# Odd rows' way back split by frequencies modulo 4, with six rows unfolded on GpSimd, and later transfers put behind the first unit's keys

## The chip, the cores and the metric

One core of a Trainium2 chip runs the whole program. The metric is the device time of one execution in microseconds (us). An execution of the kernel before takes about 453 us, so half a per cent is 2.3 us.

## The reference

The input x is 2048 x 640. Two branches work on it, and a gate per row mixes them:

```python
g = sigmoid((x * gate_w).sum(-1))
a = attention(x @ wqkv) @ wo       # 32 heads of 20; query s sees keys s, s-2, ..., s-14
b = irfft2(rfft2(x) * (w_r + 1j * w_i))
return g * a + (1 - g) * b
```

The second branch is a product in the frequency domain: 2048 points along the rows, 640 along the columns. The change touches its last step, the way back along the 640 columns, and the order of transfers ahead of the attention.

## The kernel before

**Tiles.** Row s of x lies on partition p = s // 16 with index j = s % 16, so a "row j" below is a set of 128 rows. Even and odd j have separate queries and keys, since the attention's step is 2.

**Stages.** (1) `qkv`: x times wqkv in eight units u (four column groups hg for even j, four for odd j), in fp32r with three terms each. Each pair of j goes through an `ev` tile to a buffer `qkvd` in DRAM. (2) `attend(par, h)`: 16 attention units in the order of UNITS; each loads its keys `kt`, queries `q` and values `vt` from `qkvd`. The first is kt0a/q0a/vt0a, the second kt0b (both from u = 0), the third kt4a (u = 4). VectorE multiplies and reduces (`pr`, `L`, `o`), GpSimd does softmax pieces and `pv`. Results `o` go to the DRAM buffers `od`. (3) `fold`, `cols`, `freq`: x is folded by symmetry on VectorE (`fx`; two of the folded tiles wait in DRAM as `fd`), transformed along the rows (`z`), along the columns with the table `bt` (matmuls `u`, `v`), multiplied with the weights (`X`, `P`, `s`), and brought back (`g`). (4) `project_even`: attention output of even j (load `ot`, transposes `oTp`, matmuls `woa`, `wob`), to DRAM as `ad`. (5) `spatial(j)`: the way back along the columns with the table `gt` (matmuls `oa`, `ob`, evictions `os` on ScalarE), then the last half transform (`ha`, `hb`). For even j VectorE unfolds it at once into `y`, which is added to `yi` (from `ad`) and written. For odd j ScalarE only stores the halves `ho`. (6) `project_odd(j)`: unfolds `ho` into `ye` and `y`, projects attention, adds the two and writes `out`.

**Tables and symmetry.** PERM orders the 321 column frequencies: even ones first, odd ones after. With cosine and sine parts apart, the even and the odd frequencies of a row give two halves of 161 numbers, and sums and differences of these make 321 and then 640 outputs. In `spatial` a chunk of 128 frequencies that has both kinds takes a matmul of 322 columns, one that has a single kind one of 161.

**What sets the order.** Nothing is issued as it is written. A class `Plan` records every operation, gives each a cost, and searches an order per engine by list scheduling with random trials; operations are then issued engine by engine in that order (all at one line, L655 in the profile). So each engine works through a fixed row of instructions and waits where an operand is missing. SP, ACT and POOL issue DMAs in the same rows as their other work. A change of costs or dependencies redraws the whole order. Buffers are rings of named places: `yr` holds four `y` tiles, `yer` one `ye` tile, banks 0 to 4 of PSUM hold `woa`/`wob` of odd rows.

The lines that the change turns on:

```python
ODD_POOL = tuple(range(1, 16, 2))            # odd rows that GpSimd unfolds
YI_DMA = tuple(range(0, 10, 2))              # even rows added by an accumulating DMA of GpSimd
...
op.busy = max(4 * n / 2400 + 0.006, 0.182)   # the plan's cost of an f32 matmul
...
U.tensor_add(ye[:, :, 0:161], h[:, 0], h[:, 1])
U.tensor_sub(ye[:, 0, 320:160:-1], h[:, 0, 0, 0:160], h[:, 1, 0, 0:160])
U.tensor_sub(ye[:, 1, 320:160:-1], h[:, 1, 1, 0:160], h[:, 0, 1, 0:160])
```

Of the kernel before, what the change touches and what calls it, by code (L numbers as in the profile page):

```python
# [16 lines left out]
S, D = 2048, 640  # L17
# [7 lines left out]
PERM = np.array([0, 320] + list(range(2, 320, 2)) + list(range(1, 320, 2)))  # L25
# [7 lines left out]
def dft_tables():  # L33
# [7 lines left out]
    ke, ko = PERM[:161], PERM[161:]  # L41
    kb = PERM[2:161]
# [9 lines left out]
    def half(n, *ends):  # L52
# [3 lines left out]

    bt = np.zeros((640, 642))
    bt[0:161, 0:161] = np.cos(tau * np.outer(np.arange(161), ke) / D) * half(161, 0, 160)
    bt[161:321, 161:321] = np.cos(tau * np.outer(np.arange(160), ko) / D) * half(160, 0)
    bt[321:480, 323:482] = -np.sin(tau * np.outer(np.arange(1, 160), kb) / D)  # L60
    bt[480:640, 482:642] = -np.sin(tau * np.outer(np.arange(1, 161), ko) / D) * half(160, 159)
    bt = np.concatenate(
        [bt[0:128, 0:161], bt[128:256, 0:321], bt[256:384, 161:482], bt[384:512, 321:642], bt[512:640, 482:642]], 1
    )

    j, k2 = np.arange(16), np.arange(16)
    md = np.zeros((16, 16, 2, 4, 2, 16, 4))
    mf = np.zeros((16, 2, 16, 4, 16, 2, 4))
    for g in range(16):
        for a in range(4):  # L70
            th = tau * np.outer(j, 4 * g + a + 128 * k2) / 2048
# [48 lines left out]
    d = np.arange(161)  # L120
# [5 lines left out]
    gt[0:161, 0:161] = np.cos(tau * np.outer(ke, d) / D) * ck(ke)  # L126
    gt[161:321, 161:322] = np.cos(tau * np.outer(ko, d) / D) * ck(ko) * (d < 160)
    gt[321:480, 322:483] = -np.sin(tau * np.outer(kb, d) / D) * ck(kb) * ((d > 0) & (d < 160))
    gt[480:640, 483:644] = -np.sin(tau * np.outer(ko, d) / D) * ck(ko) * (d > 0)
    gt = np.concatenate(  # L130
        [gt[0:128, 0:161], gt[128:256, 0:322], gt[256:384, 161:483], gt[384:512, 322:644], gt[512:640, 483:644]], 1
    )
    f = np.float32
    return {
        "t_fc": np.concatenate([fc, back[0].T, back[1].T], 1).astype(f),
# [7 lines left out]
class Op:  # L143
    __slots__ = ("i", "eng", "name", "call", "busy", "lat", "size", "preds", "succs", "chain", "tail", "start", "end", "early", "group", "of", "two", "rank")
# [12 lines left out]
class Plan:  # L157
# [5 lines left out]
    def __init__(self, nc):  # L163
        self.ops, self.places, self.past = [], {}, set()
        self.chain = self.group = ""
        self.rank = 0.0
# [57 lines left out]
    def record(self, eng, name, fn, a, k):  # L224
        op = Op()
        op.i, op.eng, op.name, op.chain, op.group = len(self.ops), eng, name, self.chain, self.group
        op.preds, op.succs, op.size, op.early, op.two, op.rank = set(), [], 0, False, False, 0.0
        line = sys._getframe(2).f_lineno
# [14 lines left out]
    def cost(self, op, out, ins, k):  # L243
        n = max(int(np.prod(v.shape[1:])) for v in [out] + ins[:1])
        if op.name == "dma_start":
            op.busy, op.lat = {"SP": 0.45, "ACT": 0.45, "POOL": 1.0}[op.eng], LAND
            op.size = int(np.prod(out.shape)) * 4
            op.early = not hasattr(ins[0].tensor, "tag")
            if self.rank:
                op.rank, self.rank = self.rank, self.rank - 1e3  # L250
        elif op.eng == "PE":
# [5 lines left out]
            else:  # L257
                op.busy = max(4 * n / 2400 + 0.006, 0.182)
# [23 lines left out]
    def order(self):  # L282
# [7 lines left out]
        for op in reversed(ops):  # L290
# [7 lines left out]
            last[key] = op  # L298
        span = max(op.tail for op in ops)
# [213 lines left out]
class Mixer:  # L513
# [17 lines left out]
    def places(self, pp, dr, sb):  # L531
# [35 lines left out]
        self.yr, self.yir = ring("raw3", "raw4", "e0", "ya"), n("f", 2)  # L567
# [10 lines left out]
    def work(self):  # L578
# [45 lines left out]
        self.bt, self.gt = self.one("bt", 1288, tag="e0"), self.one("gt", 1288, tag="e1")  # L624
        S.dma_start(self.bt[:, 0:1284], ins["t_bt"])
# [16 lines left out]
        p.chain = ""  # L642
        staged([self.spatial(j) for j in range(1, NJ, 2)], 2)
# [29 lines left out]
    def load_w(self, st, hg):  # L673
# [4 lines left out]
        for t in range(5):  # L678
# [80 lines left out]
    def attend(self, par, h, step=4):  # L759
# [80 lines left out]
    def fold(self, q):  # L840
# [24 lines left out]
        V.tensor_sub(o[:, :, 0:161], o[:, :, 0:161], bl)  # L865
        V.tensor_sub(f[:, :, 321:480], o[:, :, 1:160], oh[:, :, 159:0:-1])
        V.tensor_add(f[:, :, 480:640], o[:, :, 1:161], oh[:, :, 159::-1])
        V.tensor_add(f[:, :, 0:161], e, eh[:, :, 160::-1])
        V.tensor_sub(f[:, :, 161:321], e[:, :, 0:160], eh[:, :, 160:0:-1])
        self.folded[q] = f  # L870
        if q in STORED:
            p.act.dma_start(self.f_d[:, q], f)

# [26 lines left out]
    def freq(self, g):  # L900
# [25 lines left out]
        row(v[:, 0:161], 3, bt[:, 642:803], False, False)  # L926
        row(v[:, 161:321], 5, bt[:, 1124:1284], False, True)
# [3 lines left out]
        row(u, 1, bt[:, 161:482], True, False)  # L931
        row(u[:, 0:161], 0, bt[:, 0:161], False, False)
        row(u[:, 161:321], 2, bt[:, 482:642], False, True)
# [50 lines left out]
        V.tensor_sub(s[:, d0 : d0 + 319], P[:, 0, 2:], sz[:, 2:])  # L984
# [40 lines left out]
    def spatial(self, j):  # L1025
# [8 lines left out]
        mm(o1[:, 0:322], 1, gt[:, 161:483], True, False)  # L1034
        mm(o1[:, 0:161], 0, gt[:, 0:161], False, False)
        mm(o1[:, 161:322], 2, gt[:, 483:644], False, True)
        mm(o2[:, 0:322], 3, gt[:, 805:1127], True, False)
        mm(o2[:, 0:161], 2, gt[:, 644:805], False, False)
        mm(o2[:, 161:322], 4, gt[:, 1127:1288], False, True)
        os = self.osr.next(f"os{j}", 644)  # L1040
        oq = os.rearrange("p (b a d) -> p a b d", b=2, a=2)
        A.copy(oq[:, 0], o1[:, 0:322].rearrange("p (b d) -> p b d", b=2))
        A.copy(oq[:, 1], o2[:, 0:322].rearrange("p (b d) -> p b d", b=2))
        yield
        h1, h2 = self.ps((3, 4), f"ha{j}"), self.ps((5,), f"hb{j}")
        for i, h in enumerate((h1, h2)):
            for a in range(2):
                T.matmul(
                    h[:, 161 * a : 161 * a + 161],
                    self.fct[:, a],  # L1050
                    os[:, 322 * i + 161 * a : 322 * i + 161 * a + 161],
# [5 lines left out]
        if j % 2:  # L1057
            if j % 4 == 1:
                self.hpair = self.hor.next(f"ho{j}", 2, 2, 2, 161)
            h = self.hpair[:, j % 4 // 2]  # L1060
            A.mul(h[:, 0].rearrange("p b d -> p (b d)"), h1[:, 0:322], ng)
            A.mul(h[:, 1].rearrange("p b d -> p (b d)"), h2[:, 0:322], ng)
# [63 lines left out]
    def project_odd(self, j):  # L1126
# [41 lines left out]
ODD_POOL = tuple(range(1, 16, 2))  # L1168
# [68 lines left out]
```

## Time and profile before

| | |
|---|---|
| median of three runs | 453.15 us (453.03, 453.15, 455.2) |
| the profiled execution | 452.6 us, of which the span is 450.8 us |
| TensorE (PE) busy | 443.1 us |
| VectorE (DVE) busy | 393.0 us |
| GpSimd (POOL) busy | 339.3 us |
| ScalarE (ACT) busy | 217.8 us |

Busy time of TensorE is modelled from overlapping instructions, so its real price is the distance between starts, which the chain of waits shows. `PEld` is TensorE's weight load. In a line of waits the columns are the total, the count and the longest; in a line of stages each engine's busy time is followed by its instructions, and at the end stand the granted clock, the DMA engines' share and GB/s. In a line of groups the numbers are total busy us and mean ns, then the idle time ahead. In a timeline row the first number is the start, the second the duration, and square brackets hold idle time ahead and what ended it. `SPq` and `ACTq` are DMA issues. A line of transfers ends with the size and the median us from issue to landing.

### The profile page before, as it was taken

The page shows a single profiled execution, that of the slowest core. Times are in us where ns is not written, and L with a number is a line of the kernel's source. Part 1 is how long each engine was busy: PE and PEld are TensorE (multiplying, and loading weights), DVE is VectorE, ACT ScalarE, POOL GpSimd, SP SyncE. Part 2 cuts the span into 40 slices and gives each one's busy share as a digit, 9 for nine tenths or more (in the row PEclk, how much of TensorE's full clock was granted, in tenths as well). Part 3 has the DMA queues.
Part 4 walks back from the last instruction along what each step waited for, and adds up shares of the span by engine and source line. Part 5 has one row for each costly group of instructions (what it writes and reads, how often), then busy time and mean ns, then how long its engine had stood idle before and what let it go on. Part 6 is the DMA issues. An engine that isn't in the chain of part 4 may idle for free. (4 is left out here: it accounts for less than half of the span.)

```text
span 450.8 us, 7124 instructions
## 1 busy us (share of the span) xinstructions
PE 443.1 (98%) x2437; PEld 388.8 (86%) x2437; DVE 393.0 (87%) x515; ACT 217.8 (48%) x578; POOL 339.3 (75%) x296
## 2 busy tenths in 40 slices
PE   9999999999999999999999999999999999999996
PEld 5888888888888889888987887899888999999996
DVE  5465699999999999999999999999999999989442
ACT  6464264324332333444558787878664654342120
POOL 1085047789999998899559899936498977967895
PEclk9999999999999999999999999999999999999999
DMA  8998949685665839999798676867634231769842
GB/s 313 371 316 283 354 148 313 209 273 138 210 195 160 247 115 284 300 288 288 230 268 294 177 246 191 282 222 239 197 120 129 86 98 52 190 170 230 295 147 87
DMA packets 87283, 98.65 MB, mean 219 GB/s; under 512 B 20416, under 2 KB 74816, under 8 KB 87248
## 3 DMA queue, kind: packets, MB, share of 16 engines
q1 hardware_dynamic: 47616, 63.64, 44.6%
q10 hardware_dynamic: 38864, 32.86, 23.7%
q0 software_dynamic: 768, 1.71, 2.1%
q8 instruction: 19, 0.31, 0.3%
q14 instruction: 16, 0.13, 0.1%
HBM read 66.33 MB, written 30.22 MB: 214 GB/s over the span
## 5 line engine op out<-in xcount | busy, mean ns | idle before, releaser
L655 PE MATMUL qkv<-w,xo 128*128 128x480 f32 (+1 forms) x480 | 114.2, 386 | 0.0
L655 PE MATMUL qkv<-w,xe 128*128 128x480 f32 (+1 forms) x465 | 105.3, 383 | 0.0
L655 PEld LDWEIGHTS qkv<-w,xo 128*128 128x128 f32 x480 | 89.2, 189 | 13.3 <-ACT ev L655 0.2
L655 PEld LDWEIGHTS qkv<-w,xe 128*128 128x128 f32 x465 | 87.4, 188 | 15.1 <-POOL w L655 0.5
L655 ACT COPY ev<-qkv 128x480 f32<-128x480 f32 x64 | 35.6, 558 | 46.6 <-PE qkv L655 29.6
L655 PE MATMUL woa<-wo,oT 128*128 128x320 f32 x240 | 47.7, 315 | 0.3 <-ACT oT L655 0.3
L655 PE MATMUL wob<-wo,oT 128*128 128x320 f32 x240 | 47.9, 317 | 0.0
L655 PEld LDWEIGHTS woa<-wo,oT 128*128 128x128 f32 x240 | 38.0, 188 | 0.8 <-ACT oT L655 0.6
L655 PEld LDWEIGHTS wob<-wo,oT 128*128 128x128 f32 x240 | 38.1, 188 | 0.4
L655 POOL TENSOR_TENSOR P<-X,wp 128x642 f32<-128x642 f32 x16 | 25.1, 1566 | 14.9 <-ACT X L655 14.7
L655 POOL TENSOR_TENSOR w<-raw,w 128x480 fp32r<-128x480 f32 x15 | 18.0, 1239 | 19.8 <-ACT w L655 19.8
L655 POOL TENSOR_TENSOR xo<-xt,xo 128x640 fp32r<-128x640 f32 x8 | 12.4, 1573 | 21.9 <-ACT xo L655 21.9
L655 ACT CAST oT<-oTp 128x384 fp32r<-128x384 f32 (+1 forms) x32 | 13.2, 428 | 28.6 <-PE woa L655 12.0
L655 PEld LDWEIGHTS g<-mm,s 128*128 128x128 f32 x150 | 21.9, 191 | 5.3 <-issue 0.7
L655 PE MATMUL g<-mm,s 128*128 128x128 f32 x150 | 23.5, 276 | 1.0 <-DVE s L655 0.8
L655 DVE TENSOR_TENSOR oT<-oTp,oT 128x384 fp32r<-128x384 f32 (+1 forms) x32 | 15.1, 484 | 8.9 <-ACT oT L655 8.9
L655 PE MATMUL oa<-gt,zg 128*128 128x161 f32 (+1 forms) x96 | 22.8, 344 | 0.0
L655 PE MATMUL ob<-gt,zg 128*128 128x161 f32 (+1 forms) x96 | 22.7, 345 | 0.0
L655 PE MATMUL v<-bt,zc 128*128 128x321 f32 (+2 forms) x96 | 22.2, 345 | 0.4 <-ACT zc L655 0.4
L655 PE MATMUL u<-bt,zc 128*128 128x321 f32 (+2 forms) x96 | 22.1, 344 | 0.0
L655 PEld LDWEIGHTS u<-bt,zc 128*128 128x128 f32 x96 | 15.8, 190 | 2.9
L655 PEld LDWEIGHTS v<-bt,zc 128*128 128x128 f32 x96 | 15.6, 190 | 3.0 <-ACT zc L655 0.6
(305 smaller groups left out, 1091.4 us busy)
## 6 DMA issues: line engine op xcount, KB each, us to landing
qkvd<-ev ACTq DMA_DIRECT2D x32, 480.0 KB, 4.1
wp<-in_ws SPq DMA_DIRECT2D x16, 642.0 KB, 4.6
fx<-in_x SPq DMA_DIRECT2D x8, 648.0 KB, 7.3
ot<-od SPq DMA_DIRECT2D x16, 320.0 KB, 3.8
raw<-in_wqkv SPq DMA_DIRECT2D x15, 240.0 KB, 5.0
xt<-in_xT SPq DMA_DIRECT2D x8, 320.0 KB, 8.6
ad<-ya SPq DMA_DIRECT2D x8, 320.0 KB, 2.5
yi<-ad SPq DMA_DIRECT2D x8, 320.0 KB, 3.8
```

Of the source, the lines that this page charges most:

```text
L655: p.dve.memset(w, 0.0)
```

## The change

**Odd rows' way back.** PERM now puts the odd frequencies first, then those that are 2 modulo 4, then those that are 0 modulo 4. A new table `g4` (128 x 1134) is loaded to the place of `bt`. For odd j the even frequencies are taken apart once more: their two kinds give quarters of 81 numbers each, so that the six matmuls are 324, 81, 162, 324, 81 and 162 columns wide instead of 322, 161, 161, 322, 161, 161. Even j keep `gt`, rearranged (one matmul a column narrower). The other tables and the fold write the same numbers in the new order of frequencies.

**Unfolding.** A row takes seven operations instead of five. GpSimd does it for j = 1 to 11, VectorE for 13 and 15. One place of the ring of `y` tiles moves (from `e0`, which `g4` now uses, to `ev1`).

**Later transfers.** An operation recorded with `hold` may in the plan only start after the first unit's key and query loads (`keys`): the stores of `fd`, the weights of column group 2, the first unit's values, the second unit's loads. It is a rule of the plan's order, not a wait on the chip.

**Cost.** The plan's lower bound of 0.182 us for an f32 matmul is gone.

```diff
-PERM = np.array([0, 320] + list(range(2, 320, 2)) + list(range(1, 320, 2)))
+PERM = np.array([*range(1, 320, 2), *range(2, 320, 4), *range(4, 320, 4), 0, 320])
...
-                op.busy = max(4 * n / 2400 + 0.006, 0.182)
+                op.busy = 4 * n / 2400 + 0.006
...
+        for op in ops:
+            if op.hold:
+                op.preds.update(self.keys)
...
-        self.yr, self.yir = ring("raw3", "raw4", "e0", "ya"), n("f", 2)
+        self.yr, self.yir = ring("raw3", "raw4", "ev1", "ya"), n("f", 2)
...
+        self.g4 = self.one("g4", 1134, tag="e0")
+        self.p.sp.dma_start(self.g4, ins["t_g4"])
         staged([self.spatial(j) for j in range(1, NJ, 2)], 2)
...
+                p.hold = hg == 2
                 p.sp.dma_start(raw, src[t])
+                p.hold = False
...
+        p.hold = f and u == 0
         self.queue("kt").dma_start(kt..., rows(1, 0, 15), ...)
         self.queue("q").dma_start(q..., rows(0, 7, 8), ...)
+        if (par, h) == (0, 0):
+            p.keys, p.hold = p.ops[-2:], True
         self.queue("vt").dma_start(vt..., rows(2, 0, 15), ...)
+        p.hold = False
...
         if q in STORED:
+            p.hold = True
             p.act.dma_start(self.f_d[:, q], f)
+            p.hold = False
...
+        if j % 2:
+            g4 = self.g4
+            mm(o1[:, 0:324], 1, g4[:, 162:486], True, False)
+            mm(o1[:, 0:81], 2, g4[:, 486:567], False, False)
+            mm(o1[:, 162:324], 0, g4[:, 0:162], False, True)
+            mm(o2[:, 0:324], 3, g4[:, 648:972], True, False)
+            mm(o2[:, 81:162], 2, g4[:, 567:648], False, False)
+            mm(o2[:, 162:324], 4, g4[:, 972:1134], False, True)
...
-        U.tensor_add(ye[:, :, 0:161], h[:, 0], h[:, 1])
-        U.tensor_sub(ye[:, 0, 320:160:-1], h[:, 0, 0, 0:160], h[:, 1, 0, 0:160])
-        U.tensor_sub(ye[:, 1, 320:160:-1], h[:, 1, 1, 0:160], h[:, 0, 1, 0:160])
+        he, ho = h[:, 0], h[:, 1]
+        U.tensor_add(ye[:, :, 0:81], he[:, :, 0:81], he[:, :, 81:162])
+        U.tensor_sub(ye[:, :, 160:80:-1], he[:, :, 0:80], he[:, :, 81:161])
+        U.tensor_sub(ye[:, 0, 320:160:-1], ye[:, 0, 0:160], ho[:, 0, 0:160])
+        U.tensor_sub(ye[:, 1, 320:160:-1], ho[:, 1, 0:160], ye[:, 1, 0:160])
+        U.tensor_add(ye[:, :, 0:161], ye[:, :, 0:161], ho[:, :, 0:161])
...
-ODD_POOL = tuple(range(1, 16, 2))
+ODD_POOL = (1, 3, 5, 7, 9, 11)
```

Since the plan is searched anew, orders differ on every engine. Three places matter below.

**SP, the first units' keys** (`raw` are weight chunks of column groups 2 and 3, `kt` keys). Before:

```order
L655 DMA fc<-in_t_fc 128x128
L655 DMA raw_0_192<-in_wqkv 128x480
L655 DMA raw_1_194<-in_wqkv 128x480
L655 DMA raw_2_196<-in_wqkv 128x480
L655 DMA kt0a<-qkvd 128x4x300
L655 DMA kt0b<-qkvd 128x4x300
L655 DMA raw_3_198<-in_wqkv 128x480
L655 DMA raw_4_200<-in_wqkv 128x480
L655 DMA raw_0_214<-in_wqkv 128x480
L655 DMA raw_1_216<-in_wqkv 128x480
L655 DMA kt4a<-qkvd 128x4x300
```

Now:

```order
L690 DMA fc<-in_t_fc 128x128
L690 DMA kt0a<-qkvd 128x4x300
L690 DMA kt0b<-qkvd 128x4x300
L690 DMA raw_0_192<-in_wqkv 128x480
L690 DMA raw_1_194<-in_wqkv 128x480
L690 DMA raw_2_196<-in_wqkv 128x480
L690 DMA raw_3_198<-in_wqkv 128x480
L690 DMA raw_4_200<-in_wqkv 128x480
L690 DMA raw_0_214<-in_wqkv 128x480
L690 DMA kt4a<-qkvd 128x4x300
L690 DMA kt4b<-qkvd 128x4x300
L690 DMA raw_1_216<-in_wqkv 128x480
```

Three weight loads went from ahead of kt0a to behind kt0b, and one from ahead of kt4a to behind kt4b.

**POOL, from the last attention products (`pv7b`) to the first odd rows** (`y_993`/`y_994` is row 1, `ye_998`/`ye_999` row 3, `yi` the sums of even rows). Before:

```order
L655 TENSOR_TENSOR pv7a_578<-vt7a,L7a 128x8x80 x2
L655 TENSOR_TENSOR pv7b_580<-vt7b,L7b 128x8x80
L655 DMA yi_966<-y_970 128x640
L655 TENSOR_TENSOR pv7b_580<-vt7b,L7b 128x8x80
L655 TENSOR_TENSOR y_993<-ye_992 128x321
L655 TENSOR_TENSOR y_993<-ye_992 128x319
L655 TENSOR_TENSOR ye_998<-ho_889 128x2x161
L655 TENSOR_TENSOR yi_974<-yi_974,y_978 128x640
L655 TENSOR_TENSOR ye_998<-ho_889 128x160 x2
L655 TENSOR_TENSOR y_999<-ye_998 128x321
```

Now:

```order
L690 TENSOR_TENSOR pv7b_580<-vt7b,L7b 128x8x80 x2
L690 DMA yi_967<-y_971 128x640
L690 TENSOR_TENSOR yi_975<-yi_975,y_979 128x640
L690 TENSOR_TENSOR y_994<-ye_993 128x321
L690 TENSOR_TENSOR y_994<-ye_993 128x319
L690 TENSOR_TENSOR ye_999<-ho_890 128x2x81
L690 TENSOR_TENSOR ye_999<-ho_890 128x2x80
L690 TENSOR_TENSOR ye_999<-ye_999,ho_890 128x160
L690 TENSOR_TENSOR ye_999<-ho_890,ye_999 128x160
L690 TENSOR_TENSOR ye_999<-ye_999,ho_890 128x2x161
L690 TENSOR_TENSOR y_1000<-ye_999 128x321
```

The accumulating DMA of `yi` moved behind the last `pv7b`, and row 3's unfolding has five operations ahead of its `y`. Row 5 has two `yi` sums ahead of its `y`, and rows 7, 9 and 11 follow without others between.

**DVE, the end of the program** (`y_1031`/`y_1032` is row 11, `ye_1039` row 13, `y_1047`/`y_1048` row 15; a SCALAR_TENSOR_TENSOR adds the projection to `y`). Before:

```order
L655 SCALAR_TENSOR_TENSOR y_1031<-woa_1044,g,y_1031 128x320
L655 TENSOR_TENSOR oT_1049<-oTp_1051,oT_1049 128x256
L655 SCALAR_TENSOR_TENSOR y_1031<-wob_1045,g,y_1031 128x320
L655 SCALAR_TENSOR_TENSOR y_1039<-woa_1052,g,y_1039 128x320
L655 SCALAR_TENSOR_TENSOR y_1039<-wob_1053,g,y_1039 128x320
L655 SCALAR_TENSOR_TENSOR y_1047<-woa_1054,g,y_1047 128x320
L655 SCALAR_TENSOR_TENSOR y_1047<-wob_1055,g,y_1047 128x320
```

Now:

```order
L690 SCALAR_TENSOR_TENSOR y_1032<-woa_1045,g,y_1032 128x320
L690 TENSOR_TENSOR ye_1039<-ho_923 128x2x81
L690 TENSOR_TENSOR ye_1039<-ho_923 128x2x80
L690 TENSOR_TENSOR ye_1039<-ye_1039,ho_923 128x160
L690 TENSOR_TENSOR ye_1039<-ho_923,ye_1039 128x160
L690 TENSOR_TENSOR ye_1039<-ye_1039,ho_923 128x2x161
L690 TENSOR_TENSOR y_1040<-ye_1039 128x321
L690 TENSOR_TENSOR y_1040<-ye_1039 128x319
L690 TENSOR_TENSOR ye_1047<-ho_923 128x2x81
L690 TENSOR_TENSOR ye_1047<-ho_923 128x2x80
L690 TENSOR_TENSOR ye_1047<-ye_1047,ho_923 128x160
L690 TENSOR_TENSOR ye_1047<-ho_923,ye_1047 128x160
```

Fourteen unfolding operations of rows 13 and 15 came in (twelve stand ahead of row 11's second sum, the last two ahead of row 15's first). They can start only when row 11's `y` has left the `ye` tile.

More of the change, by code (lines that the diff above doesn't have):

```diff
@@ L134, in dft_tables @@
     return {
+        "t_g4": g4.astype(f),
         "t_fc": np.concatenate([fc, back[0].T, back[1].T], 1).astype(f),
@@ L143 @@
 class Op:
-    __slots__ = ("i", "eng", "name", "call", "busy", "lat", "size", "preds", "succs", "chain", "tail", "start", "end", "early", "group", "of", "two", "rank")
+    __slots__ = ("i", "eng", "name", "call", "busy", "lat", "size", "preds", "succs", "chain", "tail", "start", "end", "early", "group", "of", "two", "rank", "hold")
 class Engine:
@@ L165, in __init__ @@
         self.chain = self.group = ""
-        self.rank = 0.0
+        self.rank, self.hold, self.keys = 0.0, False, []
         self.code = {}
@@ L227, in record @@
         op.preds, op.succs, op.size, op.early, op.two, op.rank = set(), [], 0, False, False, 0.0
+        op.hold = False
         line = sys._getframe(2).f_lineno
@@ L248, in cost @@
             op.early = not hasattr(ins[0].tensor, "tag")
+            op.hold = self.hold
             if self.rank:
@@ L298, in order @@
             last[key] = op
+        for op in ops:
+            if op.hold:
+                op.preds.update(self.keys)
+                for k in self.keys:
+                    k.succs.append(op)
+                    k.tail = max(k.tail, op.tail)
         span = max(op.tail for op in ops)
@@ L925, in freq @@
         row(v, 4, bt[:, 803:1124], True, False)
-        row(v[:, 0:161], 3, bt[:, 642:803], False, False)
-        row(v[:, 161:321], 5, bt[:, 1124:1284], False, True)
+        row(v[:, 160:321], 3, bt[:, 642:803], False, False)
+        row(v[:, 0:160], 5, bt[:, 1124:1284], False, True)
         vv = self.vsr.next(f"vs{g}", 321)
```

96 lines of the change are left out of this document (58 added, 38 removed).

## The prediction

> **What bounds the kernel now.** I read the page first (span, busy time, slices), then who waited for whom on TensorE's weight loads, then the stages.
>
> ```profile
> span 450.8 us, 7124 instructions
> PE 443.1 (98%) x2437; PEld 388.8 (86%) x2437; DVE 393.0 (87%) x515; ACT 217.8 (48%) x578; POOL 339.3 (75%) x296
> PE   9999999999999999999999999999999999999996
> DVE  5465699999999999999999999999999999989442
> 74.50:335.00 260.50, 259.01 (x1400) 224.76 (x1399) 253.35 (x313) 138.62 (x379) 217.64 (x174) 1.00 0.75 229
> 335.00:412.40 77.40, 76.30 (x485) 69.81 (x485) 73.75 (x104) 36.34 (x93) 66.92 (x55) 1.00 0.48 133
> 412.40:451.00 38.60, 34.36 (x241) 33.80 (x239) 17.40 (x33) 4.73 (x12) 27.59 (x41) 0.99 0.55 176
> PEld oTp L655 <- DVE oT L655: 1.9, 4, 0.7
> PEld xc L655 <- DVE s L655: 1.2, 3, 0.8
> PEld xa L655 <- DVE p L655: 0.7, 3, 0.3
> PEld g L655 <- DVE s L655: 0.5, 1, 0.5
> ```
>
> TensorE has work from the first slice to the last, so the first price of any change is matmul time. But VectorE is as full: 253.35 of 260.50 us in the long middle stage, 73.75 of 77.40 in the next. Only in the last 38.6 us does it have room (17.40 busy), and there GpSimd (27.59) is the busier helper. The last four rows are waits of TensorE for VectorE: 4.3 us in 11 pieces, none over 0.8. So VectorE is the second bound, and whatever starts it earlier may take some of these away. All sums below go against this execution's own 452.6 us; the runs next to it, 453.03 and 453.15, lie 0.5 higher (the median is 453.15), and I add that at the end.
>
> **1. Matmuls of odd rows.** An f32 matmul is two instructions. The chain of waits gives their pitch, the weight loads their busy time:
>
> ```profile
> 338.77 0.54 PE oa L655 x2
> 339.54 0.55 PE oa L655 x4
> 274.63 0.67 PE g L655 x6
> L655 PEld LDWEIGHTS oa<-gt,zg 128*128 128x128 f32 x96 | 15.4, 189 | 1.1
> ```
>
> 322 wide: 0.54/2 = 0.27 us an instruction; 161 wide: 0.55/4 = 0.1375; 128 wide (g): 0.67/6 = 0.112. An odd row now has two matmuls of 322 and four of 161: 4 x 0.27 + 8 x 0.1375 = 2.18 us. Afterwards two of 324, two of 162 and two of 81: 4 x 0.27 + 4 x 0.1375 + 4p = 1.63 + 4p. No instruction narrower than 128 is in the trace, so p is bounded. Along the line through 161 and 128 (0.0008 us a column) p is 0.075 and a row saves 0.25 us, eight rows 2.0. If 128 wide is already as short as it gets, p = 0.112 and eight rows save 0.8; at the worst p = 0.1375 as for 161, and they save nothing; for a loss I see no reason, since the count of matmuls stays. The three widths cost the same per column within 4%, without a floor so far, but the narrowest is the dearest of them; I take p = 0.09 and **-1.5 us**. In the second stage 162 for 161 columns is under 0.1 us in all, as is the column that even rows lose.
>
> The LDWEIGHTS section of "TensorE: Matmul & The Clock Gate" in the Trainium skill speaks against my value: a weight load takes its columns over 1.2 in ns, whatever the matmul behind it, so 128 columns take 107 ns and, as an estimate from that, no instruction of a stream with a load each could be closer than 0.107 us. By it the eight rows would save 8 x (0.55 - 4 x 0.107) = 1.0 us instead of 1.5. The 0.112 of g agrees with it, but agrees with the line as well; no run here shows a shorter matmul.
>
> **2. The table g4.** One more load (567 KB) stands on SP behind the last use of bt, whose place it takes.
>
> ```profile
> gt<-in_t_gt SPq DMA_DIRECT2D x1, 644.0 KB, 6.0
> 327.24 1.25 PE L655 MATMUL u<-bt,zc 128*128 128x321 f32 x6
> 338.61 0.71 PE L655 MATMUL oa<-gt,zg 128*128 128x322 f32 x2
> ```
>
> Now 10 us lie between the end of the last u (328.5) and the first oa (338.6), and the new order keeps two projection halves and the g groups there. gt, larger, took 6.0. So the load is hidden and I cost it at nothing; without that cover it would cost 6 us once. Behind it on SP stands the ot load of even row 10, needed only after those same halves.
>
> **3. Later transfers behind the first keys.** VectorE's only long idle stretch lies ahead of unit 0:
>
> ```profile
> 49.10 1.49 DVE L655 TENSOR_TENSOR pr0a<-kt0a,qbank 128x1280 f32<-128x1280 f32 x1 [7.90 <-DMA kt0a<-qkvd]
> 40.60 0.37 ACTq L655 DMA_DIRECT2D q0a<-qkvd  x1
> 38.09 2.80 SPq L655 DMA_DIRECT2D raw<-in_wqkv  x3
> 40.98 0.47 SPq L655 DMA_DIRECT2D kt0a<-qkvd  x1
> kt0a<-qkvd SPq DMA_DIRECT2D x1, 600.0 KB, 8.0
> kt1a<-qkvd SPq DMA_DIRECT2D x1, 600.0 KB, 4.1
> kt2a<-qkvd SPq DMA_DIRECT2D x1, 600.0 KB, 6.2
> ```
>
> kt0a shares the link with three raw loads issued just ahead of it; its like takes 4.1 to 6.2 us elsewhere. It reads what unit 0's stores wrote, and q0a, which waits for the same, was issued at 40.60. Issued then, it lands at 44.7 to 46.8 instead of 49.0: VectorE starts 2.2 to 4.3 us earlier, say 3.4. But the third unit's keys stop it again:
>
> ```profile
> 61.52 6.80 SPq L655 DMA_DIRECT2D raw<-in_wqkv  x4
> 68.42 0.38 SPq L655 DMA_DIRECT2D kt4a<-qkvd  x1
> kt4a<-qkvd SPq DMA_DIRECT2D x1, 600.0 KB, 5.7
> 74.57 2.89 DVE L655 TENSOR_TENSOR pr4a<-kt4a,qbank 128x1280 f32<-128x1280 f32 x2
> ```
>
> kt4a landed at 68.42 + 5.7 = 74.1, 0.45 us before VectorE came to it. It waits for stores that TensorE's rate sets, and TensorE is not late there. VectorE, ready at about 71.2, will stand at pr4a. Two gains remain: one raw load (a quarter of the 6.80 us for four, with its waits) now goes behind kt4a, so that it may be issued some 0.7 earlier; and it may land in 4.1. So pr4a starts between 71.8 and 74.1: of the 3.4 us, 0.5 to 2.8 survive; I take **1.2**, nearer to the first, since kt4b and the q loads still follow at its heels. The delayed loads I cost at nothing: what hides them is VectorE's 25 us on unit 0 (49.10 to 74.57), in which neither vt0a nor the weights of column group 2 are asked for until late; without that cover each would cost what it comes later, some 3 us.
>
> What the 1.2 is worth to TensorE is bounded by the four rows above: nothing, or all 4.3 us (a new order draws new waits, so it may also lose a little). I take **-1.2**. TensorE's own chain would so end at 452.6 - 1.5 - 1.2 = 449.9.
>
> **4. Unfolding of odd rows.** Per row five operations become seven.
>
> ```profile
> L655 POOL TENSOR_TENSOR ye<-ho 128x160 f32<-128x160 f32 x16 | 7.2, 467 | 0.0
> L655 POOL TENSOR_TENSOR ye<-ho 128x322 f32<-128x322 f32 x8 | 6.1, 756 | 0.6
> L655 POOL TENSOR_TENSOR y<-ye 128x319 f32<-128x319 f32 x8 | 6.0, 752 | 0.0
> L655 POOL TENSOR_TENSOR y<-ye 128x321 f32<-128x321 f32 x8 | 6.0, 750 | 3.1 <-DMA yi<-y 2.5
> 410.62 1.79 POOL L655 TENSOR_TENSOR pv7b<-vt7b,L7b 128x640 f32<-128x640 f32 x1
> 414.94 1.46 POOL L655 TENSOR_TENSOR y<-ye 128x321 f32<-128x321 f32 x2 [2.53 <-DMA yi<-y]
> yi<-y POOLq DMA_DIRECT2D x5, 320.0 KB, 4.8
> 417.20 1.58 POOL L655 TENSOR_TENSOR yi<-yi,y 128x640 f32<-128x640 f32 x1
> L655 DVE TENSOR_TENSOR y<-ha,h 128x321 f32<-128x321 f32 x4 | 2.0, 494 | 0.1
> 447.33 0.55 DVE L655 SCALAR_TENSOR_TENSOR y<-wob,g,y 128x320 f32<-128x320 f32 x1 [0.78 <-PE wob L655]
> ```
>
> On GpSimd a row goes from 0.756 + 2 x 0.467 + 1.50 = 3.2 us to 4 x 0.467 + 0.756 + 1.50 = 4.1; eight rows were 25.5, six are 24.8. VectorE gets two rows: four short and three long operations, at most 7 x 0.494 = 3.5 us a row, some 2.2 if the short ones take half. Summed up that looks free, since VectorE is idle for 21 of the last 38.6 us; but it is a chain, and all rows share one ye tile. Take the end of the last pv7b, 412.4 now, as X. Now the last y ends at 447.9, X + 35.5. Afterwards the accumulating transfer of yi stands behind the last pv7b instead of before it, and the first y waits for its buffer: X + 4.8. Then row 1 takes 1.5, row 3 4.1, row 5 with two yi sums 7.3, and rows 7, 9 and 11 12.4: X + 30.1. Only then may VectorE unfold rows 13 and 15 (their ye waits for row 11's y), and behind that on its queue stand the last five y sums of 0.55: 14 operations (4.4 to 5) and 2.75, so X + 37.2 to 37.8. Neighbours overlap by up to 0.1 us (1.46 for two of 0.75), which over 43 operations may take up to 1.7 off: the chain is **0.6 to 2.3 us longer than now, say +1.3**.
>
> X itself moves: by the 1.2 of part 3; by 0.6, since one oT subtraction that stood ahead of the last reduction now stands behind; and by the wait for TensorE just before:
>
> ```profile
> DVE h L655 <- PE ha L655: 1.1, 1, 1.1
> ```
>
> TensorE has done all eight odd rows by then and comes 1.5 earlier, so this 1.1 goes too: -2.9 (ends -1.1 and -4.5). So this chain ends at 452.6 + 1.3 - 2.9 = 451.0, with ends 448.7 and 453.8.
>
> **The sum.** The kernel ends with the later chain: 451.0, not TensorE's 449.9. Plus 0.5 for the runs: **451.5 us**, a gain of 0.4%. The cheaper matmuls are real, but the last rows' unfolding eats about half.
>
> **The rivals.**
> *TensorE alone decides.* If attention ends 4 us earlier or more, because VectorE's idle 7 us in the middle stage shrink too, the tail is ahead of TensorE again, and the time is 449.9 + 0.5 or less; with all 4.3 us of waits gone and 2.0 for the matmuls 452.6 - 6.3 + 0.5 = 446.8. For it: TensorE's last row still came 0.78 after VectorE was free. I take 449.5 as its middle; 33%.
> *Slower: the tail.* kt4a lands as before, X moves by less than 0.6, and the chain is 2.3 longer: 452.6 + 2.3 - 0.6 + 0.5 = 454.8; with a GpSimd wait for a yi load of the size of today's 2.53 ahead of row 5 it is 457.3. It decides from the point where X moves less than the tail grows. Against it: every one of X's three parts has its own row. 14%.
> *No shorter matmuls and a clear tail.* p = 0.112 and no wait gone: 452.6 - 0.8 + 0.5 = 452.3; 11%, with the skill's floor of 0.107 at about the same place (452.1).
>
> **How the numbers follow.** My forecast has 42%, its own range 449.2 to 454.3 by the ends of the chain. Half a per cent is 2.3 us, about what a measurement can tell from no change: faster means under 450.9, slower over 455.4. Of the forecast most is inside (33), 8 faster, 1 slower; of the first rival 31 faster, 2 inside; of the second 8 slower, 6 inside; the third inside. Faster 39%, within 52%, slower 9%. The range of 8 in 10 leaves out the upper half of the slower rival and the best of the first: 447.8 to 455.0.
>
> **What would show it.** The 81-wide matmuls' pitch: 0.18 us a matmul right, 0.22 or more the floor. kt0a landing by 47 and a new VectorE wait for kt4a of some 2 us: part 3. In the tail, VectorE's wait for GpSimd's y of row 11 and then unfolding up to the end while TensorE is done: part 4; if instead the last y waits for TensorE, the first rival holds. A wait of TensorE for g4, or for the banks that the late y sums hold, would make me wrong altogether.

## The result and the profile after

The changed kernel takes **459.5 us** (median of 4 runs, 458.74 to 461.78) against 453.91 for the kernel before beside it (4 runs): ratio 1.0121, 95% interval 1.0097 to 1.0146. It is 1.2% slower. The forecast was 451.5 us, range 447.8 to 455.0, a small gain; the measured time lies 4.5 us above that range. The profiled execution took 458.74 us.

The page (span, busy time, slices) and the three stages after, in the columns of the prediction:

```profile
span 456.7 us, 7129 instructions
PE 443.9 (97%) x2437; PEld 388.2 (85%) x2437; DVE 399.8 (88%) x529; ACT 217.7 (48%) x578; POOL 339.8 (74%) x298
PE   8979999999999999999999999999999999999995
DVE  4546699999999999999999999999999999889446
```
```profile
74.30:335.00 260.70, 258.31 (x1382) 223.21 (x1380) 252.80 (x307) 135.75 (x371) 217.62 (x172) 1.00 0.73 228
335.00:414.60 79.60, 78.49 (x505) 71.61 (x505) 73.95 (x104) 39.69 (x102) 67.35 (x59) 1.00 0.49 134
414.60:456.00 41.40, 36.87 (x256) 36.14 (x255) 24.76 (x53) 4.88 (x12) 27.63 (x42) 0.98 0.53 170
```

Two things differ to the eye. The third slice of TensorE is a 7, where there was a 9, and the last stage, from the end of the last pv7b to the end, is 41.4 us instead of 38.6, with VectorE busy 24.8 instead of 17.4. The middle stages are alike in work.

**The hole in the third slice.** TensorE's timeline and ScalarE's between 10 and 33 us (start, duration, in brackets the idle time before and what ended it; ACTq is a DMA that ScalarE issues), and who waited for whom there:

```profile
10.64 18.97 PE L690 MATMUL qkv<-w,xe 128*128 128x482 f32 x85 [0.16 <-DVE xe L690]
32.39 3.78 PE L690 MATMUL qkv<-w,xe 128*128 128x482 f32 x16 [2.78 <-ACT z L690]
25.77 0.15 ACT L690 COPY z<-qkv 128x1 f32<-128x1 f32 x1
30.01 0.56 ACT L690 COPY ev<-qkv 128x480 f32<-128x480 f32 x1 [4.09 <-DMA qkvd<-ev]
30.46 1.35 ACT L690 CAST xo<-xt 128x640 fp32r<-128x640 f32 x2
31.72 0.56 ACT L690 COPY ev<-qkv 128x480 f32<-128x480 f32 x1
32.17 0.17 ACT L690 COPY z<-qkv 128x1 f32<-128x1 f32 x1
```
```profile
PEld qkv L690 <- ACT z L690: 3.2, 1, 3.2
```

The copy at 30.01 takes row 4 of column group 0 out of its bank into a store tile whose earlier contents are still being written out; ScalarE stands 4.09 us for that DMA. Behind it on ScalarE stands the copy of row 3 (31.72), which had what it needed. TensorE needs row 3's bank for row 7 and stops for 2.8 us. In the order before, ScalarE had row 3 first. The plan was searched anew for the changed program, and this is a draw of that search, not a part of the edit; it stood on ScalarE, an engine that the prediction did not go through.

**The first keys**, in the rows of the prediction's part 3, from the timeline and the DMA view (the last number is the us to landing):

```profile
43.46 0.44 ACTq L690 DMA_DIRECT2D q0a<-qkvd  x1
43.51 0.38 SPq L690 DMA_DIRECT2D kt0a<-qkvd  x1
48.86 1.49 DVE L690 TENSOR_TENSOR pr0a<-kt0a,qbank 128x1280 f32<-128x1280 f32 x1 [4.76 <-ACT qbank L690]
```
```profile
kt0a<-qkvd SPq DMA_DIRECT2D x1, 600.0 KB, 4.8
```

The load takes 4.8 us instead of 8.0, but it is issued 2.5 later because what it reads is written later, so VectorE starts only 0.24 us earlier than before.

**The tail.** GpSimd's and VectorE's timeline, first and last rows of it, and TensorE's last piece:

```profile
411.82 2.79 POOL L690 TENSOR_TENSOR pv7b<-vt7b,L7b 128x640 f32<-128x640 f32 x2 [2.75 <-DVE o7b L690]
419.45 1.45 POOL L690 TENSOR_TENSOR y<-ye 128x321 f32<-128x321 f32 x2
444.91 1.46 POOL L690 TENSOR_TENSOR y<-ye 128x321 f32<-128x321 f32 x2
446.41 0.56 DVE L690 TENSOR_TENSOR ye<-ho 128x162 f32<-128x162 f32 x2 [0.15 <-POOL y L690]
453.31 0.54 DVE L690 SCALAR_TENSOR_TENSOR y<-wob,g,y 128x320 f32<-128x320 f32 x1
449.15 2.37 PE L690 MATMUL wob<-wo,oT 128*128 128x320 f32 x15
```

With X the end of the last pv7b, 414.61: GpSimd ends row 11 at 446.37, X + 31.8; VectorE unfolds rows 13 and 15 from 446.41 on and ends at 453.85, X + 39.2. TensorE is done at 451.5. Before, it was X + 35.5 with X = 412.4.

### The profile page after: what moved, and what is told of

Its sections match the earlier page's. It is cut to its first block, busy times and chain, and to the rows that moved or that the text cites. A ratio compares the mean times of both kernels' runs of the same rounds, so it can differ in the third digit from the quotient of the medians.

```text
span 456.7 us, 7129 instructions
## 1 busy us (share of the span) xinstructions
PE 443.9 (97%) x2437; PEld 388.2 (85%) x2437; DVE 399.8 (88%) x529; ACT 217.7 (48%) x578; POOL 339.8 (74%) x298
## 4 chain that ended last, share of the span: by engine, by line
PE 75%; POOL 6%; DMA 6%; DVE 5%; ACT 3%; issue 2%; SPq 0%; POOLq 0%; DVEq 0%; ACTq 0%
PE qkv L690 41%; PE woa L690 4%; PE ob L690 4%; PE oa L690 4%; PE wob L690 4%; PE z L690 3%; POOL ye L690 3%; PE g L690 3%; PE u L690 2%; PE v L690 2%; PE hb L690 2%; PE ha L690 2%; DMA xt<-in_xT 2%; POOL y L690 2%; DMA st<-in_xT 1%
## 5 line engine op out<-in xcount | busy, mean ns | idle before, releaser
L690 PE MATMUL qkv<-w,xo 128*128 128x480 f32 (+1 forms) x480 | 109.4, 384 | 0.0
L690 PE MATMUL qkv<-w,xe 128*128 128x480 f32 (+1 forms) x465 | 102.9, 382 | 2.9 <-ACT z L690 2.8
L690 PE MATMUL wob<-wo,oT 128*128 128x320 f32 x240 | 45.5, 315 | 0.3 <-ACT oT L690 0.3
L690 PEld LDWEIGHTS g<-mm,s 128*128 128x128 f32 x150 | 20.5, 191 | 3.8 <-ACT zg L690 1.3
L690 PE MATMUL u<-bt,zc 128*128 128x321 f32 (+2 forms) x96 | 21.0, 344 | 0.0
L690 PEld LDWEIGHTS z<-fc,fx 128*128 128x128 f32 x120 | 15.7, 191 | 0.7
L690 PE MATMUL oTp<-ident,ot 128*128 128x128 f32 x80 | 15.3, 274 | 0.8 <-DVE oT L690 0.6
```

What stands on the lines that cost most here:

```text
L690: p.dve.memset(w, 0.0)
```

## The experiments

Kernels below keep a recorded order as a list, in which only the rows shown are moved, unless the text says otherwise.

**swap: one row of ScalarE.** The changed kernel, with the one copy set behind row 3's.

```diff
 COPY z<-qkv0_4
-COPY ev0_4_115<-qkv0_4_114
 CAST xo9<-xt9
 CAST xo11<-xt11
 COPY ev0_2_112<-qkv0_3_113
 COPY z_72<-qkv0_3_113
 DMA qkvd_64<-ev0_2_112
+COPY ev0_4_115<-qkv0_4_114
```

> The order of the kernel after, row by row, with one row of ScalarE moved: the copy of unit 0's row 4 (its ev tile waits for a store) stands behind row 3's copy and store instead of ahead of them. Theory A (one row in the redrawn order): TensorE's stop of 2.96 us at 29 us goes, kt0a lands near 45.4, VectorE's pr0a starts near 45.9 instead of 48.86, the last pv7b ends near 411.6 instead of 414.6 and the time is 456.5 us (459.5 - 3.0). Rival B (VectorE is full and its later waits set the end): TensorE runs ahead by 3 us, but pr4a waits for kt4a or other keys again and the last pv7b moves by less than 1 us; 458.5 to 459.5 us.

Measured 455.89 us (455.56 to 456.58), 1.0041 [1.0026, 1.0057] against before (454.24, 26 runs): 3.6 us of the 5.6 lost were this one row. Timeline of the swap kernel:

```profile
46.29 1.49 DVE L690 TENSOR_TENSOR pr0a<-kt0a,qbank 128x1280 f32<-128x1280 f32 x1 [4.95 <-ACT qbank L690]
408.10 2.82 POOL L690 TENSOR_TENSOR pv7b<-vt7b,L7b 128x640 f32<-128x640 f32 x2 [2.90 <-DVE o7b L690]
450.35 0.54 DVE L690 SCALAR_TENSOR_TENSOR y<-wob,g,y 128x320 f32<-128x320 f32 x1
```

X falls by 3.69 us, to 410.92, and the last y by 2.96, to 450.89. The tail is 0.7 us longer than in after (X + 40.0); in this execution the transfers of yi ahead of row 1's y landed later, the accumulating one after 5.6 us instead of 4.9. Of the 3.69 us, 0.6 lie ahead of the moved row: the copy of z on ScalarE just before it, alike in both orders, starts at 25.18 instead of 25.77. The rest is the stop, and it arrives at X undiminished: it had held up TensorE, whose next group starts at 32.76 instead of 36.45, and not VectorE alone.

**swap_loads_first: are the weight loads what slowed kt0a?** swap, with the three weight loads that the change holds back set ahead of kt0a again.

```diff
 DMA fc<-in_t_fc
+DMA raw_0<-in_wqkv
+DMA raw_1<-in_wqkv
+DMA raw_2<-in_wqkv
 DMA kt0a<-qkvd
 DMA kt0b<-qkvd
-DMA raw_0<-in_wqkv
-DMA raw_1<-in_wqkv
-DMA raw_2<-in_wqkv
```

> As swap, and on SyncE the three weight loads of column group 2 stand ahead of kt0a and kt0b again, as in the kernel before (the hold undone at that place alone). By the prediction's step on the hold: kt0a takes about 8 us instead of 4.8, pr0a starts 3 us later than in swap, and 1.2 us of it reach the end: swap + 1.2. Rival: all of it reaches the end, since VectorE is full: swap + 3. Rival: nothing, swap + 0.3 at most.

Measured 455.81 us, 1.0041 [1.0026, 1.0055]: the same as swap. In its DMA view, and then its timeline, kt0a still lands fast, with the loads ahead of it in SyncE's row:

```profile
kt0a<-qkvd SPq DMA_DIRECT2D x1, 600.0 KB, 5.0
```
```profile
47.20 1.49 DVE L690 TENSOR_TENSOR pr0a<-kt0a,qbank 128x1280 f32<-128x1280 f32 x1 [5.49 <-DMA kt0a<-qkvd]
```

This does not clear the loads. kt0a had to wait for the stores that it reads until 42.07, and the three loads, issued from 36.0 on, had landed by 42.44, so they hardly met. In the kernel before, the last of them landed at 44.92, 3.9 us after kt0a was issued. What the run does show: VectorE starts 0.9 us later than in swap, and the whole takes the same time.

**swap_unheld: then which transfers?** swap, with the order of before on SP and ScalarE around the first keys.

```diff
 ScalarE
+DMA fd
 DMA q0a<-qkvd
+DMA q0b, DMA vt0a, DMA fd
 ...
 COPY qbank x3      (before: only behind the ev4_2 copy)
 ...
-DMA q0b, DMA fd, DMA vt0a   (changed kernel: behind the ev4_2 copy; vt0b later)
 SyncE (as in swap_loads_first)
+DMA raw_0, raw_1, raw_2<-in_wqkv ahead of kt0a
```

> As swap, with the same stretch of SyncE and ScalarE put back in the order of the kernel before (the hold undone on both queues). Theory A: kt0a takes about 8 us again, pr0a starts near 49.1, and since VectorE is full all of it reaches the end: 455.9 + 2.8 = 458.7 us. By the prediction's step only 1.2 us reach it: 457.1. Rival: as in swap_loads_first nothing, 455.9.

Measured 457.84 us, 1.0074 [1.0052, 1.0096], 1.95 more than swap. DMA view and timeline:

```profile
kt0a<-qkvd SPq DMA_DIRECT2D x1, 600.0 KB, 6.8
```
```profile
49.52 1.49 DVE L690 TENSOR_TENSOR pr0a<-kt0a,qbank 128x1280 f32<-128x1280 f32 x1 [7.14 <-DMA kt0a<-qkvd]
```

So the hold is worth 2.0 us in this order. Against swap_loads_first, which has the same three weight loads ahead of kt0a, ScalarE's q0b, vt0a, vt0b and fd stores are back beside it, and the load takes 6.8 us instead of 5.0.

**before_keys: the weight loads alone, in the kernel before.** Its three weight loads behind kt0b, nothing else.

```diff
 DMA fc<-in_t_fc
-DMA raw_0_192, raw_1_194, raw_2_196<-in_wqkv
 DMA kt0a<-qkvd
 DMA kt0b<-qkvd
+DMA raw_0_192, raw_1_194, raw_2_196<-in_wqkv
```

> The order of the kernel before, row by row, with three rows of SyncE moved: the three weight loads of column group 2 stand behind kt0a and kt0b instead of ahead of them. By the prediction's step on the hold: kt0a takes 4 to 5 us instead of 8.0, pr0a starts 3.4 us earlier, pr4a 1.2 us earlier, and the time falls by 1.2 us to 452.7. Rival: VectorE waits for kt4a all the same and nothing is gained (453.9 within 0.3), or the loads, 3 us late, stop TensorE (slower).

Measured 455.88 us, 1.0034 [1.0019, 1.0048]: slower. The profiled execution is the slowest of its twelve (457.45). DMA view, then ScalarE's and VectorE's timeline:

```profile
kt0a<-qkvd SPq DMA_DIRECT2D x1, 600.0 KB, 5.6
```

```profile
47.43 0.56 ACT L655 COPY ev<-qkv 128x480 f32<-128x480 f32 x1 [7.57 <-DMA kt0a<-qkvd]
50.81 0.56 ACT L655 COPY ev<-qkv 128x480 f32<-128x480 f32 x1 [2.75 <-DMA kt0b<-qkvd]
51.31 0.97 ACT L655 COPY qbank<-q0a 128x160 f32<-128x160 f32 x3
52.32 1.49 DVE L655 TENSOR_TENSOR pr0a<-kt0a,qbank 128x1280 f32<-128x1280 f32 x1 [10.20 <-ACT qbank L655]
```

With the weight loads alone out of its way kt0a takes 5.6 us, where the four traces with the order of before around it (before, split_in_before, widths, narrow_in_before) have 7.7 to 8.0. So here the weight loads are most of what slows it. But that gives VectorE nothing: the query copies (qbank) stand on ScalarE behind two ev copies that wait for the store tile, and VectorE starts at 52.32, 3.2 later than before. (The transfer that a wait names is the one that came last by the profile; these copies need their tile's store.)

**hold_in_before: the whole hold, in the kernel before.** SP and ScalarE around the first keys as in the changed kernel, with the qbank copies right behind the first ev4_0 store; the split is left out.

```diff
 SyncE: raw_0, raw_1, raw_2 behind kt0b, as in before_keys
 ScalarE
-DMA fd
 DMA q0a<-qkvd
-DMA q0b, DMA vt0a, DMA fd
 COPY ev4_0 and its store
+COPY qbank x3
 COPY ev4_2
+DMA q0b, DMA fd, DMA vt0a
-COPY qbank x3
```

> The kernel before, row by row, with the stretch of SyncE and ScalarE around the first unit's keys put in the order of the kernel after: q0b, both fd stores, vt0a and vt0b behind q0a's copies instead of right behind q0a, and the three weight loads behind kt0b. Nothing of the split. Theory A (what the hold gives is VectorE's start, and a full VectorE passes it on): pr0a starts near 46.3 instead of 49.1 and the last pv7b ends 2.8 earlier; TensorE's waits of 4.3 us bound the gain, so the time is 452.5 to 453.3 us against 454.2. Rival (the prediction's stop at kt4a): pr4a starts less than 1.2 us earlier and the time is 453.8 to 454.3.

Measured 453.62 us against 454.25, 0.9993 [0.9974, 1.0012]: nothing to be told from no change. Timeline and VectorE's waits:

```profile
46.46 1.49 DVE L655 TENSOR_TENSOR pr0a<-kt0a,qbank 128x1280 f32<-128x1280 f32 x1 [4.68 <-ACT qbank L655]
```
```profile
DVE s5a L655 <- ACT L5a L655: 1.6, 1, 1.6
DVE pr1a L655 <- ACT qbank L655: 0.7, 1, 0.7
```

kt0a takes 4.8 us. VectorE starts 2.64 us earlier and still has 2.19 of it when it reaches the third unit (pr4a) and 2.89 at pr1a; at pr3a it is 0.41 and at the last pv7b 0.13. It is lost in waits for ScalarE and not at kt4a: the two rows shown, 1.59 and 0.65 us, which the kernel before does not have, are 2.2 of the 2.5 us lost between pr1a and pr3a. So a VectorE that is full does not pass on all that it gains ahead.

**split_in_before: the split alone.** The order of before with the split's operations set in, rows 13 and 15 unfolded on VectorE at the end.

```diff
 (order of before; two 81-wide products an odd row, g4, five operations for ye)
-POOL: ye, y of rows 13 and 15
+DVE:  ye, y of rows 13 and 15, ahead of the last five y sums
```

> The split alone in the order of the kernel before: tables, matmuls, seven operations for a row, rows 13 and 15 on VectorE at the end as in the kernel after, g4 loaded behind the last u; no hold, no other row moved. Theory A (the last rows' chain sets the end, at the sizes of the kernel after): the last y ends 39.2 us behind the last pv7b instead of 35.5: 454.2 + 3.7 = 457.9 us. By the prediction's size for that chain (1.3 longer, less 0.9 for the matmuls where TensorE decides): 455.5. Rival (TensorE decides): 454.2 - 0.9 = 453.3.

Measured 457.06 us, 1.0061 [1.0038, 1.0085]: 2.8 us slower. Its profiled execution is its slowest (458.58), so only its differences count:

```profile
412.94 1.76 POOL L690 TENSOR_TENSOR pv7b<-vt7b,L7b 128x640 f32<-128x640 f32 x1
453.24 0.54 DVE L690 SCALAR_TENSOR_TENSOR y<-wob,g,y 128x320 f32<-128x320 f32 x1
```

The tail from 414.70 to 453.78 is again X + 39.1, now in another order.

**swap_tail and swap_tail2: the tail's chain cut.** Rows 13 and 15 get a ye place of their own, free by then, so VectorE can unfold them in its idle time. In swap_tail2 only row 13 goes early.

```diff
-        ye = self.yer.next(f"ye{j}", 2, 321)
+        ye = (self.yer if j < 13 else self.yer2).next(f"ye{j}", 2, 321)
 DVE (swap_tail)
+ye13 (5 ops) behind row 9's oT, ye15 (5 ops) behind row 11's oT
+y13 behind row 13's oT, y15 behind row 15's oT
 DVE (swap_tail2)
+ye13: 2 ops behind row 9's oT, 3 behind row 11's; y13 behind row 13's oT
 ye15, y15 at the end, behind row 11's first sum
```

> As swap, and the ye tiles of rows 13 and 15 get places of their own (where keys and values of dead units lay), so that VectorE's fourteen unfolding operations can stand earlier on its queue, in four of its idle stretches between 428 and 444 us. Theory A (the end is the chain of last rows on GpSimd and VectorE): the end falls to TensorE's last matmul plus one y sum, 1.7 us below swap: 454.8 us. Rival B (something else sets the end, such as the banks or TensorE itself): within 0.5 us of swap.

> As swap_tail, but only row 13 is unfolded early (two operations ahead of row 11's oT, three behind it, the two of y later), and row 15 again at the end, when GpSimd is done. Theory A (in swap_tail the early operations took 1.1 to 1.3 us beside GpSimd instead of 0.33 and held back oT, so TensorE stood still for 1.2 us more): TensorE no longer waits and the end is 1.8 us below swap: 454.1. Rival B (any early operation costs GpSimd as much as it saves): 454.7 as swap_tail, or more.

Measured 454.73 us, 1.0013 [0.9998, 1.0028], and 454.39 us, 1.0003 [0.9987, 1.0018]: 1.2 and 1.5 less than swap, both level with before and not told from each other. In swap_tail the last y waits 1.66 us for TensorE's wob, so the tail no longer ends the kernel there, and the time is still only that of before. One reason why swap_tail falls short of the 1.7 expected can be read: VectorE's early operations run beside GpSimd. Groups on VectorE and GpSimd, of swap for the first row, of swap_tail for the others (count, busy us, mean ns):

```profile
L690 DVE TENSOR_TENSOR ye<-ho 128x162 f32<-128x162 f32 x2 | 0.7, 330 | 0.2 <-POOL y L690 0.2
```
```profile
L690 DVE TENSOR_TENSOR ye<-ho 128x162 f32<-128x162 f32 x2 | 2.2, 1096 | 0.0
L690 DVE TENSOR_TENSOR ye<-ho 128x160 f32<-128x160 f32 x2 | 2.6, 1298 | 0.0
L690 DVE SCALAR_TENSOR_TENSOR y<-wob,g,y 128x320 f32<-128x320 f32 x8 | 4.4, 546 | 2.2 <-PE wob L690 1.7 <-POOL y L690 0.5
```
```profile
PEld oTp L690 <- DVE oT L690: 1.4, 2, 0.8
```

The first two operations of a row go from 0.33 us to 1.1 and 1.3 beside GpSimd (the next two from 0.32 to 0.75, the 322-wide one from 0.49 to 0.67), and TensorE waits for an oT that stands behind them (the last row). The y sums, of which one operand is TensorE's result, keep their 0.546.

**The seeds: is it the draw?** Both programs planned anew, with another random seed in the search.

```diff
-TURNS, AGAIN, MOVE, SEED = 6, 250, 2.0, 2
+TURNS, AGAIN, MOVE, SEED = 6, 250, 2.0, 4    (and 1)
```

> The kernel after with seed 4 instead of 2 for the plan's random search: the same operations, another order. In its order ScalarE evicts unit 0's rows in turn. Theory A (1.2% of slowdown is 2.8 us of split plus a chance order): near the kernel swap, 455 to 457 us, with no stop of TensorE over 1 us near 29 us. Rival B (the change costs 5 us in any order): 458.5 to 460.5 us.

> The kernel after with seed 1. Row 6's copy stands ahead of row 5's on ScalarE, so a smaller stop of TensorE may show in unit 0 or behind it. Theory A: 455 to 458 us. Rival B: 458.5 to 460.5 us.

> The kernel before with seed 4. Theory A (orders scatter by some us, and the seed at hand was a good one for the kernel before): 454.5 to 457 us, slower than before. Rival B (the order hardly matters): 453.8 to 454.7 us.

> The kernel before with seed 1. Theory A: 454.5 to 457 us. Rival B: 453.8 to 454.7 us.

Against before (454.71, 8 runs): changed program 459.15 with seed 4, 1.0107 [1.0082, 1.0131], and 459.59 with seed 1, 1.0106 [1.0075, 1.0137]; program of before 456.9, 1.0059 [1.0036, 1.0083], and 458.67, 1.0097 [1.0071, 1.0122]. The theory that another draw would bring the changed program to 455 to 457 fails: without the stop at 29 us it loses as much elsewhere (TensorE in after_seed4 is idle for 4.8 of the 175 us from 175 to 350, in before for 2.2). But the program of before loses as well: seed 2 was a lucky draw for it. Drawn afresh, the two programs lie only about 1.6 us apart (means of two, 459.4 and 457.8), which is no more than the 1.8 between the two redraws of before. What differs can be read at the end: in both redraws of before, as in before itself, the last y waits for TensorE, here in before_seed4:

```profile
451.91 0.55 DVE L655 SCALAR_TENSOR_TENSOR y<-wob,g,y 128x320 f32<-128x320 f32 x1 [1.67 <-PE wob L655]
```

In the three draws of the changed program, the tail on GpSimd and VectorE ends it, at X + 39.2 to 39.4.

**widths: the floor of a matmul.** The kernel before, with 84 additional f32 matmuls behind its last sum, 12 for each width (two instructions each).

```diff
+for n in (32, 64, 81, 96, 112, 128, 161):
+    for i in range(12):
+        p.pe.matmul(b[:, 0:n], self.ident, self.gt[:, 0:n], start=True, stop=True)
```

> The kernel before, row by row, with 84 f32 matmuls added behind its last row: twelve each of 32, 64, 81, 96, 112, 128 and 161 columns, results unused. Theory A (a floor near 0.107 us an instruction): 32 to 112 wide all start 0.106 to 0.110 us apart, 128 near 0.11, 161 at 0.136. Rival B (the line through 161 and 128): 0.03 at 32 wide, 0.055 at 64, 0.07 at 81.

The chain of waits, for 32 wide, then in part of the 81-wide (at half clock) and of the 128-wide piece, and the granted clock (last but two) in the second:

```profile
449.99 2.88 PE width L659 x24
457.90 3.20 PE width L659 x15
473.45 1.79 PE width L659 x16
```
```profile
456.00:459.00 3.00, 2.94 (x15) 2.75 (x14) 0.00 (x0) 0.00 (x0) 0.00 (x0) 0.50 0.00 0
```

128 wide: 1.79/16 = 0.112 us an instruction; 32 wide, with the end of the last: 0.120, by starts 0.111 to 0.112; 161 wide 0.137. Below 128 columns an instruction gets no shorter. At granted clock 0.50, 81 wide: 3.20/15 = 0.213; 81 and 96 wide ran at half clock alone here, and 81 wide at full clock is in the trace of after (below, part 1).

**narrow_in_before: the gain of the matmuls alone.** The kernel before, in which two products of each odd row leave out 80 of 161 columns.

```diff
-mm(o1[:, 0:161], 0, gt[:, 0:161], False, False)
+n = 81 if j % 2 else 161
+mm(o1[:, 0:n], 0, gt[:, 0:n], False, False)
```

> The kernel before, row by row, in which two of an odd row's four 161-wide matmuls take 81 columns: the other 80 columns of these products are left out, so part of the odd rows' way back is missing. Unfolding, tables and order are those of before. Theory A (TensorE decides the end of the kernel before, the floor is 0.109): 8 x 4 x (0.1375 - 0.109) = 0.9 us less, 453.5 against 454.4. Rival (VectorE's and GpSimd's chain decides there): 454.4 within 0.3.

Measured 454.13 us against 454.52, 0.9988 [0.9965, 1.001]: at most 1.6 us gained, nothing that can be told from zero. It stays open whether the 0.8 us of shorter matmuls reach the end.

## Why the prediction was wrong, step by step

**The bound.** Right in kind: TensorE and VectorE are both full, and the chain of the last rows ended the kernel, as the likeliest case had it. Wrong in what I searched: I read the moved rows of SP, GpSimd and VectorE, and not ScalarE's, where one row costs 3.6 us. The sum has no term for it.

**Part 1, matmuls: mis-sized.** Booked -1.5 us at 0.09 an instruction; it was 0.112. In the chain of waits of after, two 81-wide and two 162-wide:

```profile
364.27 0.50 PE ob L690 x4
```

0.50 instead of 0.55, sixteen times: 0.8 us. The row of g (128 wide, 0.112) was the floor, not a point of a line that goes on. On the weight loads, the section LDWEIGHTS of "TensorE: Matmul & The Clock Gate" in the Trainium skill was the better guide than my line: its 107 ns stand beside the measured 111 to 112 at full clock (at granted clock 0.50 it was 213).

**Part 2, g4: right.** In after the load (g in the profile) was issued at 330.97 and took 4.6 us; the first matmul that reads it starts at 344.10.

**Part 3, the hold: right in the load and in most of its cause, wrong in what follows.** kt0a did take 4.8 us. In the order of before, the weight loads that I blamed are most of what slowed it (before_keys: 5.6 instead of 8.0). The transfers that ScalarE issues beside it are the rest, and I had left them out: 0.8 us there (hold_in_before: 4.8), 1.8 in the order of after (swap_unheld against swap_loads_first). Each of these is one execution. "VectorE, ready at about 71.2, will stand at pr4a" failed: in hold_in_before it kept 2.19 us there, since kt4a was issued 2.1 us earlier as well (66.31 instead of 68.42). The gain was lost behind it, in waits for ScalarE, so that 1.2 booked was nothing measurable in before's order, 2.0 in after's. In the profiled execution of after, the stop at 29 us had eaten it ahead of pr0a.

**Part 4, the tail: mis-sized, and X wrong.** Here the sum failed. X was to fall by 2.9, to 409.5; it is 414.6, 5.1 later than predicted. Of this 3.7 go with the stop (swap: 410.9; 0.6 of them lie ahead of the moved row). The other 1.4 are missing from the three gains that made up the 2.9. In swap, VectorE is 2.1 us ahead of before at pr7a (343.17 against 345.25), more than part 3's 1.2, but only 1.5 at X. The wait of 1.1 for ha is gone there, as booked; in its place VectorE waits 1.5 us for GpSimd's pv7b in swap and in after, and 0.9 for ScalarE's oT. In after:

```profile
397.19 1.49 DVE L690 TENSOR_REDUCE o7b<-pv7b 128x160 f32<-128x1280 f32 x1 [1.50 <-POOL pv7b L690]
```

So the new order took one wait away and brought others, for which the sum had no term. What the oT subtraction that moved behind X gave, no run shows. From X on, row 1 (X + 6.3), row 5 (7.4 us) and VectorE's two rows (7.4) came as worked out. GpSimd's rows 3, 7, 9 and 11 did not: 4.5 us instead of 4.1 a row. GpSimd's groups by form from 414 us on:

```profile
L690 POOL TENSOR_TENSOR ye<-ye,ho 128x322 f32<-128x322 f32 x5 | 4.1, 816 | 0.4
L690 POOL TENSOR_TENSOR ye<-ho,ye 128x160 f32<-128x160 f32 x5 | 2.7, 532 | 0.0
L690 POOL TENSOR_TENSOR ye<-ho 128x160 f32<-128x160 f32 x5 | 2.4, 471 | 0.0
```

The new operations that read ye and write it take 0.53 and 0.82 us, where I had taken the 0.467 and 0.756 of operations that read only ho. That is 0.2 us a row, 1.0 us for the five rows up to row 11's y. There the chain is 1.7 late; the other 0.7 are pauses of about 0.07 us between operations, four a row instead of two. Before, a row took 3.22 us from y to y for 3.19 us of work, now 4.51 for 4.32. And the overlap of neighbours, for which I took another 0.7 off, did not come (with all of it the low end of my range would have been 0.0, not the 0.6 I wrote: 37.2 - 1.7 - 35.5). Together 2.4. With X's 5.1, that is 7.5 of the 7.7 us between 451.0 and 458.74.

**The 0.5 for the runs: too small.** The profiled execution of before, 452.6 us, lies 1.6 under the median of its later runs (454.24).

**The rivals.** "TensorE alone decides" and "a clear tail" failed: TensorE is done 2.3 us ahead of the end. "Slower: the tail" had the right mechanism, at 454.8; split_in_before gives the split alone +2.8 us. It had 14%, and deserved more: its tail of +2.3 was the upper end that I halved (measured: 39.2 - 35.5 = 3.7), and the decrease of X, which I held against it, rested on three gains that all had to come.

By medians, then: the split +2.8; the hold between -0.6 (not told from zero) and -2.0; ScalarE's one row +3.6. The parts don't add up to the 5.6 exactly, because each depends on the order that it stands in.

## What to carry to other kernels

Where an edit makes a planner draw the order anew, price the draw first: go through every engine's rows for an operation that waits long (a copy into a tile still being stored) ahead of one that another engine needs, the nominally idle engine too. A chain of dependent small operations on a busy helper is priced operation by operation, from rows with the same operands, in place or not, with the pauses between them and without credit for overlap. And a gain upstream of a full engine is kept only if that engine waits for nothing else behind it; here 2.6 us at 46 us were 0.1 at 412.

## What the runs showed of the hardware

f32 matmul instructions, each with a weight load of 128 columns, do not start closer than 0.111 us from 32 to 128 columns, and at granted clock 0.50 they start 0.213 apart: this floor goes with the clock. In the widths run TensorE issued matmuls of 32 and then 64 columns without a pause from 450 us on; the granted clock fell between 453 and 456 us (0.74 there) and was 0.50 until 471. Why was not tried.

In swap_tail, VectorE's 160- to 162-column operations with both operands in SBUF took 0.75 to 1.3 us instead of 0.33 while GpSimd worked, GpSimd's 319-column y rose from 0.75 to 0.82, and VectorE's sums with one operand from TensorE did not change. The section "Who interferes with whom" of "SBUF — State Buffer" in the Trainium skill has this as an exclusive lock on a port pair that VectorE and GpSimd share; the numbers here agree with VectorE being held for whole GpSimd instructions: in swap_tail, two VectorE operations of 0.33 us took 2.96 while two GpSimd sums of 1.6 us ran.

```profile
426.26 2.96 DVE L690 TENSOR_TENSOR ye<-ho 128x162 f32<-128x162 f32 x2
425.85 3.19 POOL L690 TENSOR_TENSOR yi<-yi,y 128x640 f32<-128x640 f32 x2
```

At the end of after and swap, where GpSimd is done, the same operations take 0.33 or less, and the prediction's duration for them held.
